# Phase 1 of a transformer block: the normalised input turned by DMA transposes of 16-bit planes in place of TensorE transposes

## The chip, the cores and the metric

The kernel runs on one core of one Trainium2 chip. The metric is the time of one execution on the device in microseconds (us), as the median of the runs shown. A profiled execution of the same kernel gives a trace, and the views quoted below are taken from it. PE is TensorE (PEld its weight loads), DVE is VectorE, ACT is ScalarE, POOL is GpSimd and SP is SyncE, whose queue issues most of the DMAs.

## What is computed

A block with 2048 tokens of width 640, 32 heads of 20 features, and a condition vector `c`:

```python
sa, ca, ga, sb, cb, gb = silu(c) @ w_mod, cut into six rows of 640
h = layernorm(x) * (1 + ca) + sa
q, k, v = h @ wqkv
phi(t) = concat(softmax(t @ w_phi), softmax(-(t @ w_phi)))      # per head
o = phi(q) (phi(k)^T v) / (phi(q) sum(phi(k)) + 1e-6)
x = x + ga * (o @ wo)
h = layernorm(x) * (1 + cb) + sb
out = x + gb * (relu(h @ w1 + b1)**2 @ w2 + b2)
```

The change is in the first line with `h`: in how the normalised x, tokens on the partitions, becomes h with its features on the partitions, as the products with wqkv need it.

## The kernel before, in words

All products are made in fp32r with both factors split into a high and a low part, and three products per pair (`three`, line 84). The tokens lie in 16 tiles of 128, worked on in eight pairs j of 256.

Phase 1 makes k, v and q of all tokens and sums phi(k)^T v. A first stretch, ordered by hand, deals with pairs 0 and 1 of tokens as far as their normalised x and h (lines 147 to 700). The loop of lines 713 to 761 then runs over the tiles t = 2 to 13, where j, i = divmod(t, 2). In each round TensorE makes k of the tile (`proj("k", t)`, line 718), v (line 727), in even rounds the sums of the two tiles before (`do_kv`, lines 729 and 730), and q (line 746; the q of the last four tiles comes later). A projection is 30 matmuls, 15 of them 384 columns wide and then 15 of 256: for each of the five chunks d of the features, three. The loop for the 384 columns already runs over all five chunks (lines 403 to 405), so a projection needs the last chunk of h after 12 matmuls.

Beside that, the loop readies the next pair, j + 1. `load_x` loads it two pairs ahead (line 716). `ln_parts` (line 331) normalises it in place in the tile `xb`, in the even round, in three steps: ACT sums the rows, ACT sums the squares with POOL working out the factors (lines 338 and 343 to 345), and ACT scales the two halves of the tile (line 348). Then `t1` (line 383) makes h of the pair: `t_in` (line 355) lets TensorE turn two blocks of 128 x 128 per chunk into the PSUM bank `tp`, and `t_out` (line 365) has ACT scale and shift them into a row `hfa` (line 368), ACT write the high part `hT` (line 369) and DVE the low part (line 88). Chunks 0 and 1 are turned at the end of the even round (line 756), chunks 2 and 3 in the odd round between v and q (line 742), chunk 4 inside q of the odd round (line 746). In three of these rounds `t1` also takes `more`: a block of a modulation row is turned on TensorE as well (`mod_turn`, line 300). For pair 7 the places are other ones, as tiles 12 and 13 make no q in the loop: line 720, line 530 by way of line 732, and line 727.

In this loop only TensorE's order is that of the program (`pe = tc.manual_schedule(engines={ET_.PE})`, line 711). What ACT, DVE, POOL and SP do is ordered by the compiler's planner, which works with its own estimate of each operation's time. `issue_after` binds some of it: `k_norm` of a round follows the DVE work written before it (line 743), and in odd rounds `q_chain` (spread, exponentials and sums of q) follows the low part of chunk 4 (`DONE[1]`, line 751). Each engine, and SP with its DMAs, works its queue in order: an instruction that waits holds all behind it.

Buffers that matter: rows of the tag `s3` (three of them, line 48) hold `junk` of `ln_parts` and `hfa`; the tiles `x0` and `x1` hold the normalised pairs alternately; `h0` and `h1` hold h.

Phase 2 (attention and the product with wo, lines 766 to 1221) and phase 3 (the MLP, from line 1224) are not touched.

Of the kernel before, what the change touches and what calls it, by code (L numbers as in the profile page):

```python
# [8 lines left out]
F32 = mybir.dt.float32  # L9
F32R = mybir.dt.float32r  # L10
I32 = mybir.dt.int32
AF = mybir.ActivationFunctionType
ALU = mybir.AluOpType
AX = mybir.AxisListType

P = 128
# [5 lines left out]
NT = S // P  # L22
NC = D // P
# [28 lines left out]
def kernel(  # L52
# [19 lines left out]
    nc = tc.nc  # L72
# [44 lines left out]
    def row(tag, name):  # L117
        return (pc if tag in ("s3", "s4") else mem).tile([P, D], F32, tag=tag, name=name, bufs=BUFS[tag])
# [19 lines left out]
    def tp(name):  # L138
        return psA.tile([P, 512], F32, tag="tp", name=name)
# [69 lines left out]
    raw, WM, RV, XB = {}, {}, {}, {}  # L209
# [18 lines left out]
    def flat(e):  # L228
        return e.rearrange("p s d -> p (s d)")
# [101 lines left out]
    def ln_parts(xt, nm, spare=None):  # L331
        sm = small([P, 2], "sm", f"sm{nm}")
        sq = small([P, 2], "sq", f"sq{nm}")
        nb = small([P, 2], "nb", f"nb{nm}")
        for i in range(2):
            same = spare[i] if spare else xt[:, i] if nm[0] == "a" else row("s3", f"same{nm}_{i}")
            nc.scalar.activation(same, xt[:, i], AF.Identity, accum_out=sm[:, i : i + 1])
        nc.gpsimd.tensor_scalar(sm, sm, -1.0 / D, None, op0=ALU.mult)
        yield
        for i in range(2):  # L340
            junk = spare[i] if spare else row("s3", f"junk{nm}_{i}")
            nc.scalar.activation(junk, xt[:, i], AF.Square, bias=sm[:, i : i + 1], accum_out=sq[:, i : i + 1])
        nc.gpsimd.tensor_scalar(sq, sq, 1.0 / D, EPS, op0=ALU.mult, op1=ALU.add)
        nc.gpsimd.tensor_tensor(sq, sq, mhalf, op=ALU.pow)
        nc.gpsimd.tensor_tensor(nb, sm, sq, op=ALU.mult)
        yield
        for i in range(2):
            nc.scalar.activation(xt[:, i], xt[:, i], AF.Identity, bias=nb[:, i : i + 1], scale=sq[:, i : i + 1])
        yield

    def layer_norm(xt, nm, spare=None):
        for _ in ln_parts(xt, nm, spare):
# [2 lines left out]
    def t_in(xn, d, p):  # L355
        for i in range(2):
            nc.tensor.transpose(p[:, i * P : (i + 1) * P], xn[:, i, d * P : (d + 1) * P], ident)  # L357
# [23 lines left out]
    DONE = []  # L381

    def t1(j, *ds, more=None):
        if 0 in ds:
            HT[j] = ht(f"hT{j}", j)
        p = tp(f"ta{j}_{ds[0]}")
        for k, d in enumerate(ds):
            t_in(XB[j], d, p[:, 256 * k : 256 * k + 256])
        if more:
            mod_turn(more[0], p[:, 256:], 4)  # L390
        for k, d in enumerate(ds):
            t_out(cols_a, HT[j], d, f"a{j}", p[:, 256 * k : 256 * k + 256])
        DONE[:] = newest(ET_.Activation), newest(ET_.DVE)
        if more:
            mod_sum(*more)
# [126 lines left out]
    def wo_weights(*gs):  # L522
# [4 lines left out]
        6: lambda: mod_turn(2, tp("mc2"), 0, 1, 2, 3),  # L527
        8: lambda: mod_turn(3, tp("mc3"), 0, 1, 2, 3),
        10: lambda: mod_turn(4, tp("mc4"), 0, 1, 2, 3),
        12: lambda: t1(NT // 2 - 1, 2, 3),  # L530
    }
    gate_a = const.tile([P, NC], F32, name="gate_a")
    gate_b = const.tile([P, NC], F32, name="gate_b")
# [179 lines left out]
    for t in range(2, NT - 2):  # L713
        j, i = divmod(t, 2)
        if i == 0 and j < NT // 2 - 2:
            load_x(j + 2)
        PK[t] = row("s2", f"k{t}")
        to_sb(proj("k", t), PK[t])
        if t == NT - 4:
            t1(j + 1, 0, 1)  # L720
        norm = j + 1 if i == 0 and t < NT - 4 else j + 2 if t == NT - 5 else None
        if norm:
            if not i:
                parts = ln_parts(XB[norm], f"a{norm}")
            with tc.issue_after(newest(ET_.Activation)):
                next(parts)
        p = proj("v", t, (1, 0, lambda: t1(j + 1, 4)) if t == NT - 3 else None)
        if i == 0:
            do_kv(t - 2)
            do_kv(t - 1)  # L730
            if t in AFTER_KV:
                AFTER_KV[t]()
        v_out(t, p)
        if norm and not i:
            next(parts)
        EK[t] = tok2("k", f"ek{t}")
        spread(PK[t], EK[t], f"k{t}")
        exps(EK[t])
        if norm and not i:
            next(parts)  # L740
        if i and t < NT - 4:
            t1(j + 1, 2, 3)
        with tc.issue_after(newest(ET_.DVE)):
            k_norm(EK[t], t)
        if t < NT - POSTPONED:
            do_q(t, (1, 3, lambda: t1(j + 1, 4, more=LAST_COL.get(t))) if i else None)
            if norm and i:
                with tc.issue_after(newest(ET_.Activation)), tc.issue_after(DONE[0]):
                    next(parts)
            if i:  # L750
                with tc.issue_after(DONE[1]):
                    q_chain(t)
            else:
                q_chain(t)
        if i == 0 and t < NT - 4:
            t1(j + 1, 0, 1)
        if t == NT - 6:
            parts = ln_parts(XB[j + 2], f"a{j + 2}")
            with tc.issue_after(newest(ET_.Activation)):
                next(parts)  # L760
        SIDE[t]()
# [941 lines left out]
```

## Time and profile before

| what | value |
|---|---|
| time, median of 3 runs | 766.31 us (765.49 to 766.42) |
| the profiled execution's own time | 766.05 us |
| its span, first to last instruction | 764.3 us |
| granted TensorE clock | 1.000 |
| TensorE's busy share of the span | 99% |
| the loop of phase 1 (tiles 2 to 13) in the span | about 52 to 224 us |

The span is what the views cut up; the 1.75 us between it and the profiled execution's own time lie around it. A row of the timeline gives start, length, engine, line, operation and how many instructions were merged. In the grouped views the mean length of one instruction stands in ns. A row of the view of a line has the shortest, the median and the longest duration.

### The profile page before, as it was taken

The page shows a single profiled execution, that of the slowest core. Times are in us where ns is not written, and L with a number is a line of the kernel's source. Part 1 is how long each engine was busy: PE and PEld are TensorE (multiplying, and loading weights), DVE is VectorE, ACT ScalarE, POOL GpSimd, SP SyncE. Part 2 cuts the span into 40 slices and gives each one's busy share as a digit, 9 for nine tenths or more (in the row PEclk, how much of TensorE's full clock was granted, in tenths as well). Part 3 has the DMA queues.
Part 4 walks back from the last instruction along what each step waited for, and adds up shares of the span by engine and source line. Part 5 has one row for each costly group of instructions (what it writes and reads, how often), then busy time and mean ns, then how long its engine had stood idle before and what let it go on. Part 6 is the DMA issues. An engine that isn't in the chain of part 4 may idle for free.

```text
span 764.3 us, 15303 instructions
## 1 busy us (share of the span) xinstructions
PE 758.5 (99%) x5968; PEld 739.7 (97%) x5968; DVE 593.9 (78%) x1083; ACT 435.6 (57%) x972; POOL 144.9 (19%) x301
## 2 busy tenths in 40 slices
PE   9999999999999999999999999999999999999997
PEld 8999999999999989988999999999999999999997
DVE  6598897988999899999655667876767666685666
ACT  5766756677853364546776647465563645536331
POOL 3001101001100255432101000231321313213110
PEclk9999999999999999999999999999999999999999
DMA  8811431343332345223366466996766759767460
GB/s 322 329 61 78 138 104 54 104 136 112 126 104 93 109 150 188 72 87 104 122 194 221 120 227 236 283 334 209 224 166 207 232 179 268 199 184 204 126 184 35
DMA packets 51505, 126.69 MB, mean 166 GB/s; under 512 B 6684, under 2 KB 7457, under 8 KB 51433
## 3 DMA queue, kind: packets, MB, share of 16 engines
q1 hardware_dynamic: 34098, 84.65, 32.8%
q0 software_dynamic: 14752, 35.76, 16.9%
q10 hardware_dynamic: 2583, 5.30, 1.8%
q8 instruction: 47, 0.77, 0.5%
q14 instruction: 25, 0.20, 0.1%
HBM read 95.70 MB, written 29.89 MB: 164 GB/s over the span
## 4 chain that ended last, share of the span: by engine, by line
PE 91%; DVE 7%; DMA 1%; issue 0%; SPq 0%; ACT 0%; DVEq 0%
PE up L78 24%; PE acc L78 18%; PE pq L78 9%; PE pk L78 9%; PE pv L78 9%; PE pwo L78 6%; PE acc3x L78 5%; PE kvp L450 3%; PE te L920 1%; DVE dn L878 1%; DVE scr L876 1%; DVE ezb L900 1%; PE tb L357 1%; PE ta L357 1%; DVE ot L88 1%; PE foldq L280 1%
## 5 line engine op out<-in xcount | busy, mean ns | idle before, releaser
L78 PE MATMUL up<-h,w 128*128 128x256 f32 x1640 | 206.4, 278 | 0.0
L78 PEld LDWEIGHTS up<-h,w 128*128 128x128 f32 x1640 | 196.1, 188 | 0.0
L1255 ACT ACTIVATE ft<-up,b_t 128x256 f32<-128x256 f32 x104 | 49.1, 472 | 113.8 <-PE up L78 113.2
L78 PE MATMUL acc<-w,ra 128*128 128x384 f32 x452 | 97.4, 335 | 0.0
L1256 DVE TENSOR_TENSOR ft<-ft 128x256 f32<-128x256 f32 x104 | 44.1, 424 | 48.4 <-ACT ft L1255 46.8
L78 PE MATMUL pwo<-wo,ot 128*128 128x256 f32 (+3 forms) x512 | 80.5, 312 | 0.1
L78 PEld LDWEIGHTS pwo<-wo,ot 128*128 128x128 f32 (+1 forms) x512 | 74.4, 188 | 3.2 <-issue 2.7
L78 PE MATMUL pq<-wq,hT 128*128 128x384 f32 (+1 forms) x480 | 75.2, 312 | 0.0
L78 PEld LDWEIGHTS acc<-w,ra 128*128 128x128 f32 x452 | 72.7, 188 | 0.8 <-DVE ra L88 0.5
L78 PE MATMUL pk<-wk,hT 128*128 128x384 f32 (+1 forms) x480 | 72.7, 308 | 0.0
L78 PE MATMUL pv<-wv,hT 128*128 128x384 f32 (+1 forms) x480 | 71.7, 307 | 0.0
L78 PEld LDWEIGHTS pq<-wq,hT 128*128 128x128 f32 x480 | 71.1, 188 | 0.6 <-issue 0.2
L78 PEld LDWEIGHTS pk<-wk,hT 128*128 128x128 f32 x480 | 70.5, 188 | 0.4 <-issue 0.2
L78 PEld LDWEIGHTS pv<-wv,hT 128*128 128x128 f32 x480 | 70.1, 188 | 0.0
L88 DVE TENSOR_TENSOR ra<-ft,ra 128x384 fp32r<-128x384 f32 (+2 forms) x86 | 36.8, 449 | 32.6 <-ACT ra L1279 19.3
L1365 POOL DMA_DIRECT2D ring_a<-td_a x34 | 18.3, 539 | 126.1 <-PE acc L78 100.4
L1279 ACT ACTIVATE ra<-ft 128x384 fp32r<-128x384 f32 x48 | 25.2, 526 | 28.4 <-DVE ft L1256 22.4
L78 PE MATMUL acc3x<-w,ra 128*128 128x256 f32 x231 | 39.8, 278 | 0.0
L78 PEld LDWEIGHTS acc3x<-w,ra 128*128 128x128 f32 x231 | 37.2, 188 | 0.2 <-DVE ra L88 0.2
L1270 DVE TENSOR_TENSOR ft<-ft 128x128 f32<-128x128 f32 x136 | 33.4, 287 | 1.2
L441 DVE TENSOR_REDUCE sk<-ek 128x64 f32<-128x1280 f32 x16 | 23.7, 1484 | 12.4 <-ACT ek L436 10.8
L884 POOL TENSOR_TENSOR dn<-dn,rs_q 128x32 f32<-128x32 f32 x32 | 20.2, 630 | 66.7 <-DVE dn L878 66.4
(270 smaller groups left out, 1412.6 us busy)
## 6 DMA issues: line engine op xcount, KB each, us to landing
ring_c<-td_c POOLq DMA_DIRECT2D x34, 384.0 KB, 4.2
ring_a<-td_a POOLq DMA_DIRECT2D x34, 384.0 KB, 4.1
ring_b<-td_b POOLq DMA_DIRECT2D x34, 256.0 KB, 4.0
esp<-eq SPq DMA_DIRECT2D x12, 640.0 KB, 3.0
el<-esp SPq DMA_DIRECT2D x12, 640.0 KB, 3.9
rw<-in_w SPq DMA_DIRECT2D x23, 320.0 KB, 2.9
wm<-in_w_mod SPq DMA_DIRECT2D x20, 320.0 KB, 3.3
xb<-in_x SPq DMA_DIRECT2D x8, 640.0 KB, 4.2
```

The lines of the kernel that those rows point to most:

```text
L78: nc.tensor.matmul(o, a, b, start=first and i == 0, stop=last and i == len(terms) - 1, skip_group_check=skip,)
L88: (eng or nc.vector).tensor_tensor(out_lo, full, hi.bitcast(F32), op=ALU.subtract)
L280: nc.tensor.matmul(p[g // 3][:, (g % 3) * 120 : (g % 3) * 120 + n], r, bd_t[:120, g * 120 : g * 120 + n], start=True, stop=True,)
L357: nc.tensor.transpose(p[:, i * P : (i + 1) * P], xn[:, i, d * P : (d + 1) * P], ident)
L441: nc.vector.tensor_reduce(s, heads(flat(e)), axis=AX.X, op=ALU.add)
L450: nc.tensor.matmul(kvp[g // 4][64 * c : 64 * c + 64, a : a + 2 * n].rearrange("p (s n) -> p s n", s=2), v[:, u], e[:, :, o : o + n], start ...
L884: nc.gpsimd.tensor_tensor(dn[:, s], dn[:, s], rs[:, 1 - s], op=ALU.mult)
L1255: nc.scalar.activation(r, p, AF.Relu, bias=b1_t[:, f : f + 1])
L1256: nc.vector.tensor_tensor(r, r, r, op=ALU.mult)
L1270: nc.vector.tensor_tensor(t[:, o], t[:, a], t[:, b], op=op)
L1279: nc.scalar.activation(a[:, 0, :3], t[:, :3], AF.Copy)
L1365: nc.gpsimd.dma_start(RING[j, n, r], TD[n][r].bitcast(F32R))
```

## The change

`ln_parts` of a pair that belongs to phase 1's loop (pairs 2 to 7) ends with `by_dma`. The normalised tile is read as 16-bit numbers, and POOL copies the lower and the upper halves of all numbers into two planes for each of the two token tiles: four copies of 128 x 640 numbers with a step of two. Four DMA transposes from SP's queue then turn each plane, 128 tokens x 640 features, into five blocks of 128 x 128, written back over the normalised tile. In `t1` POOL joins the two planes of a chunk into a row `hfa`, two copies of 128 x 256 numbers with a step of two in what is written, and `t_out` works on that row in place, reading SBUF where it read PSUM. TensorE turns nothing of x in the loop. `t1` for chunks 0 and 1 moves from the end of the even round to the odd round, behind the copies of k; pair 7's chunks 0 to 3 all move to the odd round t = 13. The blocks of the modulation rows are still turned on TensorE, in a PSUM tile of their own and ahead of the chunk's work.

```diff
+    def by_dma(j, xt):
+        raw = flat(xt).bitcast(U16)
+        halves = raw.rearrange("p (i d h) -> p i h d", i=2, h=2)
+        turned = raw.rearrange("p (h b t) -> p h b t", h=2, b=NC)
+        planes = [row("s3", f"pl{j}_{i}").bitcast(U16).rearrange("p (h d) -> p h d", h=2) for i in range(2)]
+        for i in range(2):
+            for h in range(2):
+                nc.gpsimd.tensor_copy(planes[i][:, h], halves[:, i, h])
+        for i in range(2):
+            for h in range(2):
+                nc.sync.dma_start_transpose(turned[:, h, :, i * P : i * P + P], planes[i][:, h])
+        TURNED[j] = turned
...
     def t1(j, *ds, more=None):
+        if more:
+            mod_turn(more[0], tp(f"mc{j}")[:, 256:], 4)
         if 0 in ds:
             HT[j] = ht(f"hT{j}", j)
-        p = tp(f"ta{j}_{ds[0]}")
-        for k, d in enumerate(ds):
-            t_in(XB[j], d, p[:, 256 * k : 256 * k + 256])
-        if more:
-            mod_turn(more[0], p[:, 256:], 4)
-        for k, d in enumerate(ds):
-            t_out(cols_a, HT[j], d, f"a{j}", p[:, 256 * k : 256 * k + 256])
+        for d in ds:
+            hf = row("s3", f"hfa{j}_{d}")[:, :256]
+            for h in range(2):
+                nc.gpsimd.tensor_copy(hf.bitcast(U16).rearrange("p (t h) -> p h t", h=2)[:, h], TURNED[j][:, h, d])
+            t_out(cols_a, HT[j], d, f"a{j}", hf, hf)
...
-        if t == NT - 4:
+        if i:
             t1(j + 1, 0, 1)
+            if t == NT - 3:
+                t1(j + 1, 2, 3)
...
-        if i == 0 and t < NT - 4:
-            t1(j + 1, 0, 1)
```

More of the change, by code (lines that the diff above doesn't have):

```diff
@@ L11 @@
 I32 = mybir.dt.int32
+U16 = mybir.dt.uint16
 AF = mybir.ActivationFunctionType
@@ L348, in ln_parts @@
             nc.scalar.activation(xt[:, i], xt[:, i], AF.Identity, bias=nb[:, i : i + 1], scale=sq[:, i : i + 1])
+        if nm[0] == "a":
+            by_dma(int(nm[1:]), xt)
         yield
+    TURNED = {}
+    def by_dma(j, xt):
[10 more added lines that the diff above has]
+        TURNED[j] = turned
     def layer_norm(xt, nm, spare=None):
@@ L529 @@
         10: lambda: mod_turn(4, tp("mc4"), 0, 1, 2, 3),
-        12: lambda: t1(NT // 2 - 1, 2, 3),
     }
```

## The prediction

> **What bounds the kernel now.** I read the page first, then the stretch between two pairs (tiles 4 and 5, which make ready pair 3) by engine, then TensorE's timeline in it.
>
> ```profile
> span 764.3 us, 15303 instructions
> PE 758.5 (99%) x5968; PEld 739.7 (97%) x5968; DVE 593.9 (78%) x1083; ACT 435.6 (57%) x972; POOL 144.9 (19%) x301
> PEclk9999999999999999999999999999999999999999
> ```
>
> TensorE is busy from end to end, at full clock. So a microsecond taken off TensorE comes off the time, as long as nothing else becomes late. That is the question of this change, and it is decided in the loop. The next two views are of one round of it, by engine, and of the tile `ta` (the transposes) alone: busy times of PE, PEld, DVE, ACT, POOL in the first, of PE, PEld, ACT in the second.
>
> ```profile
> 81.90:111.70 29.80, 29.80 (x236) 29.58 (x235) 26.81 (x35) 19.57 (x44) 2.84 (x4) 1.00 0.35 114
> 81.90:111.70 29.80, 1.58 (x10) 1.16 (x10) 2.60 (x5) 1.00 0.35 114
> ```
>
> DVE is at 26.81 of 29.80 us: nearly as full as TensorE. POOL is almost empty. TensorE's own order there:
>
> ```profile
> 81.79 4.46 PE L78 MATMUL pk<-wk,hT 128*128 128x384 f32 x30
> 86.09 4.46 PE L78 MATMUL pv<-wv,hT 128*128 128x384 f32 x30
> 90.48 2.54 PE L450 MATMUL kvp<-ek,vt 128*64 128x120 f32 x44
> 92.95 4.65 PE L78 MATMUL pq<-wq,hT 128*128 128x384 f32 x30
> 97.44 0.60 PE L357 MATMUL ta<-ident,xb 128*128 128x128 f32 x4
> 97.79 4.62 PE L78 MATMUL pk<-wk,hT 128*128 128x384 f32 x30
> 102.25 4.47 PE L78 MATMUL pv<-wv,hT 128*128 128x384 f32 x30
> 106.56 0.60 PE L357 MATMUL ta<-ident,xb 128*128 128x128 f32 x4
> 106.91 3.22 PE L78 MATMUL pq<-wq,hT 128*128 128x384 f32 x18
> 109.97 0.38 PE L357 MATMUL ta<-ident,xb 128*128 128x128 f32 x2
> 111.60 0.68 PE L78 MATMUL pk<-wk,hT 128*128 128x384 f32 x3
> ```
>
> **Taken off TensorE.** From one pair's first k to the next is 111.60 - 81.79 = 29.81 us. A projection with no transposes at it takes 86.09 - 81.79 = 4.30, the sums of kv 92.95 - 90.48 = 2.47; six projections and one kv are 28.27. Left over are 1.54 us. The projection ahead of kv is 0.09 over 4.30 (90.48 - 86.09), and I leave as much for the one behind it; both stay. The ten transposes with what they disturb therefore cost 1.54 - 0.18 = 1.36 us per pair, bounded by their weight loads alone (1.16) and by all of it (1.54). Six pairs: **-8.2 us** (-7.0 to -9.2). The modulation blocks still turned (lines 305 and 306) stay as they are. The pair's period without transposes is 29.81 - 1.36 = 28.45 us.
>
> **The deadline.** Count from a pair's first k (81.79 = 0). The next pair's k would start at 28.45. The last chunk of h is needed after 12 of its 30 matmuls; 384 columns take 4.30 x 384 / 9600 = 0.172 us each, so 2.06 later: **30.5**. Before, this chain was ACT's scaling, a short turn on TensorE, ACT and DVE, with time to spare. Now it holds POOL, SP and the DMA engines.
>
> **The chain, step by step.** Its beginning and its end have rows (start, length; shortest/median/longest for the lines):
>
> ```profile
> 93.25 1.74 ACT L348 ACTIVATE xb<-xb,nba,sqa 128x640 f32<-128x640 f32 x2 [0.95 <-POOL nba L345]
> L368 ACT ACTIVATE hfa<-ta,cols_a x30: 555/564/578, 68.3 to 222.4; 128x256 f32<-128x256 f32 x30
> L369 ACT ACTIVATE hT<-hfa x40: 407/417/431, 20.9 to 223.1; 128x256 fp32r<-128x256 f32 x40
> 109.30 0.76 DVE L88 TENSOR_TENSOR hT<-hfa,hT 128x256 fp32r<-128x256 f32 x2
> 111.59 0.42 DVE L88 TENSOR_TENSOR hT<-hfa,hT 128x256 fp32r<-128x256 f32 x1
> ```
>
> *Start.* The first half is scaled at 93.25 + 0.87 = 94.12, that is 12.3; the second 0.87 later, hidden by POOL's first copies.
>
> *Four copies into planes.* No row shows such a copy. The rows around it on POOL:
>
> ```profile
> L489 POOL MEMSET rwo<- x5: 627/632/637, 152.8 to 188.7; 128x640 f32 x5
> L338 POOL TENSOR_SCALAR sma<-sma x6: 217/226/579, 58.4 to 192.2; 128x2 f32<-128x2 f32 x6
> L882 POOL TENSOR_SCALAR dd<-dd x16: 289/290/1410, 59.3 to 359.2; 128x32 f32<-128x32 f32 x16
> L884 POOL TENSOR_TENSOR dn<-dn,rs_q x32: 248/254/1481, 258.2 to 361.2; 128x32 f32<-128x32 f32 x32
> L884 POOL TENSOR_TENSOR dn<-dn,rs_q 128x32 f32<-128x32 f32 x32 | 20.2, 630 | 66.7 <-DVE dn L878 66.4
> ```
>
> Writing 640 numbers takes 0.63 us: the lower end. With one input, 30 numbers more cost 290 - 226 = 64 ns, 2.1 ns each, so 640 would take 1.6 us: the upper end. I take 0.9, near the memset, which has the length of this copy. To it comes a wait: L884 has a median of 254 ns and a mean of 630, with a longest of 1481, so on average it stood 0.38 us; I take 0.3. Four copies: 4 x 1.2 = **4.8 us** (2.5 to 7.6).
>
> *Four DMA transposes* of 160 KB each. No row shows one. Nearest are an ordinary store of 640 KB and small loads of 150 KB (KB each, us to landing):
>
> ```profile
> esp<-eq SPq DMA_DIRECT2D x12, 640.0 KB, 3.0
> rwo<-in_wo SPq DMA_DIRECT2D x10, 150.0 KB, 2.6
> ```
>
> If the four run together like one plain transfer: 3.0 us. If each waits for the one before: 4 x 2.6 = 10.4. I take **6 us**, between them, since SP must issue four and the last two wait for POOL's last copies. [...]
>
> *Ten copies that join*, 256 numbers each, all ahead of the last chunk: by the memset's rate 256 / 640 x 0.63 = 0.25, by the other row 0.22 + 254 x 2.1 ns = 0.75. I take 0.42 and the same wait of 0.3: **7.2 us** (2.5 to 10.5).
>
> *Last chunk through ACT and DVE:* 0.56 + 0.42 + 0.42 = 1.4, the same as before but now at the chain's end; and 1.2 for standing behind others there (half an ACT operation of 0.8 and a whole one of DVE): **2.6 us** (1.4 to 4). That ACT reads SBUF instead of PSUM I count at nothing: the same ACT group, off TensorE's path unless late.
>
> Sum: 12.3 + 4.8 + 6 + 7.2 + 2.6 = 32.9, **2.4 us after the deadline**. TensorE's order is fixed, so it stands and does nothing else. Per pair that is 2.4 - 1.36 = +1.04. This holds for pairs 2 to 6. Pair 7 is normalised earlier against its use:
>
> ```profile
> 203.21 1.72 ACT L348 ACTIVATE xb<-xb,nba,sqa 128x640 f32<-128x640 f32 x2
> 223.80 2.41 PE L78 MATMUL pk<-wk,hT 128*128 128x384 f32 x13
> ```
>
> There 204.1 + 4.8 + 6 + 7.2 + 2.6 = 224.7 against 223.80 - 1.36 + 2.06 = 224.5: on time, -1.2. Total 5 x 1.04 - 1.2 = **+4.0 us**.
>
> **What else is queued.** POOL waits at a join until the DMA has landed; behind it stand only `ln_parts` of the next round and a few memsets, not due yet. DVE is worse off: `k_norm` and `q_chain` of the odd round are bound behind the low parts of chunks 3 and 4. These ended at 110.06 and 112.01 (28.3 and 30.2); they move to about 31 to 33, while 26.81 us of DVE's work per pair must still fit. The wait of TensorE lengthens the period to about 30.9, so this is covered in the forecast; it isn't if the chain comes in time (third rival). On SP the transposes stand in a queue that already stops:
>
> ```profile
> 91.08 12.08 SPq L314 DMA_DIRECT2D wm<-in_w_mod  x3
> ```
>
> The third of these loads waits for its buffer until DVE has freed it. It is written in the program behind the round's transposes, so I count nothing; if it is put ahead of them, they go out at 103.2 instead of about 97, 6 us later.
>
> **Rivals.**
>
> 1. *In time.* POOL's copies at memset's rate and the DMA like one plain store: 12.3 + 3.7 + 3.0 + 5.5 + 2.6 = 27.1, well before 30.5 (waits of 0.3 included). Then all 8.2 us are gained: **758**, up to 763 with a little left on DVE. For it speaks the nearly empty POOL, against it that every unknown must be near its lower end. This ends on the other side; it decides at a chain 1.36 us past the deadline, 31.9.
>
> 2. *Later still.* The four DMAs one after the other (10.4), POOL's copies at the one-input row's rate (7.6 and 10.5): 12.3 + 7.6 + 10.4 + 10.5 + 2.6 = 43.4, 12.9 past the deadline, 5 x 11.5 - 1 = +57 at worst; with only the DMAs so, 37.3 and +26; halfway to that, with SP's load ahead now and then, **780 to 795**. The row of 12.08 us on SP speaks for it. [...]
>
> 3. *DVE becomes the bound.* The chain is in time, but POOL's 14 copies per pair hold DVE up. What the rows show is the other direction: POOL's operation of 254 ns took up to 1481 while DVE worked. Would DVE be stopped as well?
>
> ```profile
> L443 DVE TENSOR_TENSOR ek<-ek,sk x16: 1480/1486/1493, 45.7 to 243.6; 128x1280 f32<-128x1280 f32 x16
> ```
>
> Not so far: the long one never varies, but POOL had little to do beside it. DVE's operations with two inputs in this round are 20:
>
> ```profile
> L296 DVE SCALAR_TENSOR_TENSOR wm<-wm,cs,wm 128x640 f32<-128x640 f32 x4 | 3.5, 880 | 0.0
> L433 DVE TENSOR_TENSOR ek<-k,mxk 128x640 f32<-128x640 f32 x4 | 3.1, 818 | 0.0
> L433 DVE TENSOR_TENSOR eq<-q,mxq 128x640 f32<-128x640 f32 x4 | 3.0, 802 | 0.0
> L443 DVE TENSOR_TENSOR ek<-ek,sk 128x1280 f32<-128x1280 f32 x2 | 3.0, 1488 | 0.0
> L88 DVE TENSOR_TENSOR hT<-hfa,hT 128x256 fp32r<-128x256 f32 x6 | 2.3, 417 | 0.0
> ```
>
> If a quarter of them meets a copy under way (4 x 0.9 + 10 x 0.42 = 7.8 us of 28.45) and waits 0.3 to 0.5 us, that is 1.5 to 2.5: DVE needs 28.3 to 29.3, and 0.5 to 1.4 us of gain are left per pair, **759 to 763**; with DVE idle behind a low part for another microsecond, up to **768**. [...]
>
> 4. *It doesn't do what it says:* the transposes on TensorE are gone by the diff, so this can only be the order on SP, counted in 2.
>
> **How the numbers follow.** The profiled execution took 766.05 us (span 764.3), 0.26 under the median of 766.31; both give the same change. Forecast 766.3 + 4.0 = **770.3 us**. Chances: late by about this much (768 to 778) 0.30; in time, gain nearly whole (757 to 763) 0.27; near break-even, by DVE or a chain just late (763 to 768) 0.17; late by more (778 to 795) 0.18; over 795 0.08. Within 0.2%, 1.5 us, is about what a measurement can't tell from no change. Of the break-even case 0.08 lies under, 0.08 within and 0.01 over. Faster 0.35, same 0.08, slower 0.57. The range runs from the whole gain, 758, to 790.
>
> **What would show it.** Right: per pair a pause of 1 to 4 us on TensorE at the first k of pairs 3 to 6, ended by DVE or ACT on `hT`, none at pair 7, and joins on POOL released by the transposes' DMA. The plane copies should stand near 0.9, the joins near 0.4, the DMAs land some 6 us after the last plane. Wrong: no pause and a period near 28.5 (rival 1); pauses over 5 us (2); DVE without idle time and long DVE operations beside POOL's copies (3). A DMA transpose of over 4 us each, or under 1, breaks the middle step.

## The result, and the profile after

The changed kernel takes 785.16 us (median of five runs, 784.04 to 786.42) against 766.32 us before (five runs, 765.49 to 766.89): ratio 1.0249, 95% interval 1.0234 to 1.0264. It is slower, by 18.8 us where 4.0 were forecast. The profiled execution took 786.42 us, the longest of the five; its span is 784.7 - 764.3 = 20.4 us over the one before.

The page of the changed kernel, two lines of its head and the weight loads of k (busy time, mean ns of one | idle time just before them and what ended most of it); below it the same group in the view of groups of the kernel before:

```profile
span 784.7 us, 15359 instructions
PE 766.1 (98%) x5908; PEld 739.8 (94%) x5908; DVE 601.6 (77%) x1083; ACT 437.1 (56%) x972; POOL 196.7 (25%) x385
L79 PEld LDWEIGHTS pk<-wk,hT 128*128 128x128 f32 x480 | 76.4, 207 | 20.1 <-DVE hT L89 13.4
```

```profile
L78 PEld LDWEIGHTS pk<-wk,hT 128*128 128x128 f32 x480 | 70.5, 188 | 0.4 <-issue 0.2 <-ACT hT L369 0.2
```

Sixty matmuls are gone, as meant, and yet PE is busy 7.6 us longer than before (758.5). The weight loads of k show both reasons. They wait 20.1 us in place of 0.4, mostly for DVE's low part of h. And one of them lasts 207 ns in place of 188, though each does the same as before. The loads overlap one another (480 x 207 ns are 99.4 us, in 76.4 of busy time), so 480 x 19 ns is not a time lost. The granted clock of the whole execution, 0.988 in place of 1.000, has the cause: TensorE stood at half its clock in four stretches of 17.1 us together, which cost at most 8.5 us. The last 1.58 us of the span are at half clock too, but TensorE's last matmul had ended 2.5 us before them. The account nearly closes: 19.7 + 8.5 - 8.2 forecast for the turns = 20.0 us, against the 20.4 between the spans.

Where it happens is seen by cutting out the k projections that follow each pair's change (window, length, busy PE, PEld, DVE, ACT, POOL, then the granted clock): pairs 2 to 6 with the k of their first tile, pair 7 with its two k, which stand together. The row of the kernel before is pair 2's.

```profile
81.23:89.99 8.76, 7.16 (x32) 5.60 (x31) 6.68 (x11) 3.60 (x8) 1.21 (x3) 0.82 0.43 135
114.40:121.62 7.22, 5.89 (x32) 4.21 (x31) 5.68 (x9) 3.71 (x10) 1.31 (x4) 1.00 0.47 142
146.46:155.06 8.60, 6.50 (x33) 5.68 (x31) 7.40 (x11) 3.52 (x9) 1.01 (x3) 0.80 0.41 136
179.93:186.33 6.40, 5.17 (x33) 4.17 (x31) 5.12 (x8) 2.94 (x8) 0.42 (x2) 1.00 0.38 123
211.13:223.29 12.16, 8.07 (x32) 6.52 (x31) 9.52 (x15) 8.57 (x19) 7.17 (x13) 0.72 0.64 173
238.97:251.78 12.81, 11.19 (x63) 10.16 (x61) 10.28 (x14) 4.60 (x10) 0.78 (x1) 0.87 0.19 54
```

```profile
81.79:86.09 4.30, 4.30 (x32) 4.30 (x31) 4.01 (x7) 1.62 (x3) 0.00 (x0) 1.00 0.52 176
```

Each length less 4.30 is what a pair lost there (pair 7: less 8.69, as 232.49 - 223.80 before). Length times what the clock lacks is the clock's share; the rest is waiting:

| pair | forecast | lost | by the clock | by waiting |
|---|---|---|---|---|
| 2 | 2.4 | 4.46 | 1.58 | 2.88 |
| 3 | 2.4 | 2.92 | 0 | 2.92 |
| 4 | 2.4 | 4.30 | 1.72 | 2.58 |
| 5 | 2.4 | 2.10 | 0 | 2.10 |
| 6 | 2.4 | 7.86 | 3.40 | 4.46 |
| 7 | 0 | 4.12 | 1.67 | 2.45 |
| sum | 12.0 | 25.8 | 8.4 | 17.4 |

In pair 6 the clock's share is set too high and the waiting too low, by up to 0.7 us, since TensorE's weight loads also waited 1.4 us while the clock stood at half. Between these projections the changed kernel is faster, as meant, but by 0.97 to 1.27 us per pair, 6.9 in all, not 8.2. From the loop's first k (52.39, before 51.98) to the kv products after pair 7 (251.78, before 232.49) that makes 25.8 - 6.9 = 18.9 us. Of the other 1.5, 0.4 lie ahead of the loop and 1.1 behind it; these weren't followed up.

What TensorE's timeline of the k in pair 2 shows of its waits is only a part:

```profile
81.23 1.20 PE L79 MATMUL pk<-wk,hT 128*128 128x384 f32 x6
82.80 2.50 PE L79 MATMUL pk<-wk,hT 128*128 128x384 f32 x8 [0.37 <-ACT hT L387]
86.53 3.66 PE L79 MATMUL pk<-wk,hT 128*128 128x384 f32 x16 [1.23 <-DVE hT L89]
```

The eight matmuls of the second row would take some 1.3 us; more short waits hide in its 2.50, and the weight loads show them. After them the clock is at exactly one half from 86.82 to 90.23 us: 3.41 us, 1.7 lost, on top of the wait. Pair 3 waited as long (2.92 us for 2.88) and kept the full clock, so between these two the length of the waits doesn't decide.

What differs can be read from the trace. The four stretches at half clock begin at 86.82, 151.67, 216.52 and 243.83 us and last 3.41, 3.41, 6.83 and 3.41 us; between their beginnings lie 19, 19 and 8 times 3.413 us. So in this trace the clock changes only on a grid of 3.413 us, which the waits between don't shift. These are the windows of that grid in which most of each pair's waiting lies, and two stretches at half clock behind such windows (columns as above; the fourth figure is the time in which weight loads ran):

```profile
83.40:86.82 3.42, 2.19 (x9) 1.19 (x9) 3.00 (x5) 1.20 (x3) 0.00 (x0) 1.00 0.69 192
86.82:90.23 3.41, 3.41 (x17) 3.41 (x17) 3.41 (x5) 0.49 (x2) 0.00 (x0) 0.50 0.00 0
117.54:120.95 3.41, 2.17 (x14) 1.67 (x14) 3.38 (x6) 0.63 (x2) 0.00 (x0) 1.00 0.51 180
148.26:151.67 3.41, 1.49 (x7) 1.11 (x8) 3.38 (x7) 1.26 (x3) 0.00 (x0) 1.00 0.56 192
182.39:185.80 3.41, 2.18 (x15) 1.76 (x15) 3.38 (x6) 0.54 (x2) 0.00 (x0) 1.00 0.38 152
213.11:216.52 3.41, 0.98 (x6) 0.35 (x4) 1.60 (x2) 3.35 (x9) 3.27 (x8) 1.00 0.42 104
216.52:223.35 6.83, 6.02 (x23) 5.42 (x24) 6.48 (x10) 3.24 (x6) 3.63 (x6) 0.50 0.69 194
240.42:243.83 3.41, 1.78 (x8) 0.89 (x7) 2.56 (x5) 1.70 (x4) 0.00 (x0) 1.00 0.37 152
```

The four windows with the fewest weight loads, 0.35, 0.89, 1.11 and 1.19 us (pairs 6, 7, 4 and 2), are the four that half clock follows; after those with 1.67 and 1.76 us (pairs 3 and 5) the clock stays. The 19 traces of this case, cut on their own grids, have 4228 windows at full clock. Half clock follows all 24 with under 1.20 us of weight loads and none of the 4184 with over 1.55; in between, 10 of 20. So pair 3's 2.92 us of waiting, cut in two by the grid (weight loads of 2.15 us in 114.12 to 117.54, then the 1.67), were free of this cost, and pair 2's 2.88 us, more of them inside one window (2.49 us in 79.99 to 83.40, then the 1.19), cost 1.7 us more.

Now the chain that was forecast, in pair 2 (first k at 52.39): POOL, then SP, then DVE's low parts.

```profile
64.57 2.71 POOL L363 COPY pl<-xb 128x640 uint16<-128x640 uint16 x4 [1.02 <-ACT xb L349]
71.65 1.46 POOL L409 COPY hfa<-xb 128x256 uint16<-128x256 uint16 x2 [4.36 <-DMA xb<-pl]
73.52 1.73 POOL L409 COPY hfa<-xb 128x256 uint16<-128x256 uint16 x4 [0.40 <-DMA xb<-pl]
80.63 1.81 POOL L409 COPY hfa<-xb 128x256 uint16<-128x256 uint16 x4 [5.38 <-DVE hT L89]
65.99 6.11 SPq L366 DMA_TRANSPOSE xb<-pl  x4
80.15 0.42 DVE L89 TENSOR_TENSOR hT<-hfa,hT 128x256 fp32r<-128x256 f32 x1
86.11 0.36 DVE L89 TENSOR_TENSOR hT<-hfa,hT 128x256 fp32r<-128x256 f32 x1
```

Three chunks are joined by 75.25, 22.9 us after the first k and sooner than forecast. Then POOL stands for 5.38 us: the joins of chunks 3 and 4 need a row of `s3`, there are three, and the first comes free when DVE's low part of chunk 0 ends, at 80.57. That one is late because ACT takes chunk 0 only at 77.46, behind exponentials and the copies of v. DVE's last low part ends at 86.47.

Pair 7 (POOL's factors, planes and first join, then SP):

```profile
212.84 2.19 POOL L409 COPY hfa<-xb 128x256 uint16<-128x256 uint16 x4 [4.34 <-DVE hT L89]
215.11 0.19 POOL L344 TENSOR_SCALAR sqa<-sqa 128x2 f32<-128x2 f32 x1
218.55 2.91 POOL L363 COPY pl<-xb 128x640 uint16<-128x640 uint16 x4 [1.23 <-ACT xb L349]
230.23 2.04 POOL L409 COPY hfa<-xb 128x256 uint16<-128x256 uint16 x1 [8.77 <-DMA xb<-pl]
220.77 1.94 SPq L366 DMA_TRANSPOSE xb<-pl  x1
226.21 0.33 SPq L498 DMA_DIRECT2D esp<-eq  x1
226.63 1.68 SPq L366 DMA_TRANSPOSE xb<-pl  x1
```

Its factors (215.11) stand in POOL's queue behind a join of pair 6 that waits 4.34 us for a row, so its planes start only at 218.55; k, late by then itself, starts 20.4 us after that (238.97), where 19.7 lay between the first half's scaling and k before. Then its transposes stand on SP behind a store `esp<-eq` at 226.21, 3.5 us after the first transpose had left SP, and the first join comes 8.77 us after the last plane, where pair 2 needed 4.37.

### The profile page after: what moved, and what is told of

It is laid out like the page before. It is cut to its first block, busy times and chain, and to the rows that moved or that the text cites. A ratio compares the mean times of both kernels' runs of the same rounds, so it can differ in the third digit from the quotient of the medians.

```text
span 784.7 us, 15359 instructions
## 1 busy us (share of the span) xinstructions
PE 766.1 (98%) x5908; PEld 739.8 (94%) x5908; DVE 601.6 (77%) x1083; ACT 437.1 (56%) x972; POOL 196.7 (25%) x385
## 4 chain that ended last, share of the span: by engine, by line
PE 68%; DVE 16%; ACT 6%; issue 5%; DMA 2%; POOL 1%; SPq 1%; DVEq 0%; POOLq 0%; ACTq 0%
PE up L79 23%; PE acc L79 17%; PE pwo L79 5%; PE acc3x L79 5%; PE pk L79 4%; PE pq L79 4%; PE pv L79 3%; DVE sk L459 2%; DVE ek L451 2%; DVE eq L451 1%; PE te L937 1%; DVE dn L895 1%; DVE scr L893 1%; DVE ezb L917 1%; PE tb L375 1%
## 5 line engine op out<-in xcount | busy, mean ns | idle before, releaser
L79 PE MATMUL pk<-wk,hT 128*128 128x384 f32 (+1 forms) x480 | 86.1, 335 | 12.0 <-DVE hT L89 8.4
L79 PEld LDWEIGHTS pk<-wk,hT 128*128 128x128 f32 x480 | 76.4, 207 | 20.1 <-DVE hT L89 13.4
L409 POOL COPY hfa<-xb 128x256 uint16<-128x256 uint16 x60 | 34.0, 619 | 47.5 <-DMA xb<-pl 28.4
L1296 ACT ACTIVATE ra<-ft 128x384 fp32r<-128x384 f32 x48 | 25.2, 526 | 28.4 <-DVE ft L1273 22.4
L444 ACT ACTIVATE k<-pk 128x384 f32<-128x384 f32 (+1 forms) x32 | 13.6, 436 | 46.0 <-PE pk L79 46.0
```

The source lines that it names most:

```text
L79: nc.tensor.matmul(o, a, b, start=first and i == 0, stop=last and i == len(terms) - 1, skip_group_check=skip,)
L409: nc.gpsimd.tensor_copy(hf.bitcast(U16).rearrange("p (t h) -> p h t", h=2)[:, h], TURNED[j][:, h, d])
L444: nc.scalar.activation(t[:, a:b], p[h][:, : b - a], AF.Copy)
L1296: nc.scalar.activation(a[:, 0, :3], t[:, :3], AF.Copy)
```

## The experiments

Three theories at first. **O**, order and rows: each step is cheap, but in-order queues and the three rows of `s3` hold the chunks up. **D**: the DMA transposes are too long. **P**: POOL's copies and DVE's operations hold each other up. From the run with the stores issued by ACT on, O is sharpened to "the queues": an instruction that waits holds all behind it, as the store at 226.21 us held pair 7's transposes on SP. Times are medians, ratios against the kernel before on the same chip.

**One row for the joins of a call of `t1`** (the changed kernel, otherwise as it is).

```diff
+        both = row("s3", f"hfa{j}_{ds[0]}")
-        for d in ds:
-            hf = row("s3", f"hfa{j}_{d}")[:, :256]
+        for k, d in enumerate(ds):
+            hf = both[:, 256 * k : 256 * k + 256]
```

> The changed kernel, with the chunks of one call of t1 side by side in one row of tag s3 (two of 256 numbers) instead of a row each; nothing else. Theory O (order and rows: the DMA and GpSimd's copies are early enough; the joins of chunks 3 and 4 wait for a row that DVE's low part of an earlier chunk has to free, and ACT and DVE take up the chunks late): the joins of chunks 3 and 4 no longer wait for DVE's hT, some 2 us per pair come back, 773 to 779 us. Theory D (the DMA transposes take too long): 785 as before. [...]

778.82 us, 1.0162 (1.0145 to 1.018): 12.7 us over the kernel before in place of 18.8. But the weight loads of k still wait 18.8 us in place of 20.1, so the rows were little of the waiting. The clock was more: 6.8 us at half in this profile in place of 17.1, worth up to 5.1 us. Pair 7's joins are the latest.

**The changed kernel without its four DMA transposes** (the joins read the normalised tile as it lies; h isn't turned).

```diff
-        for i in range(2):
-            for h in range(2):
-                nc.sync.dma_start_transpose(turned[:, h, :, i * P : i * P + P], planes[i][:, h])
-        TURNED[j] = turned
+        TURNED[j] = raw.rearrange("p (d t h) -> p h d t", d=NC, h=2)
```

> The changed kernel with the four DMA transposes per pair left out: the joins read the normalised tile as it lies, so h is not turned (this part of the computation is changed). All copies on GpSimd and all work on ACT and DVE stay. Theory D: the cause is gone, 757 to 763 us. Theory O: the joins come about 5 us earlier per pair, but ACT and DVE still take the chunks up late and rows are still short: 775 to 785. Theory P: 780 to 785.

775.70 us, 1.013 (1.0105 to 1.0155). Without a single transpose in the chain the kernel is still 9.6 us slower than before. D falls as the main cause: at most half of the loss hangs on the DMAs, and of the waiting at k much less, as 17.3 of the 20.1 us stay.

**The kernel before with `t1` at the changed kernel's places**, turned by TensorE.

```diff
-        if t == NT - 4:
+        if i:
             t1(j + 1, 0, 1)
+            if t == NT - 3:
+                t1(j + 1, 2, 3)
...
-        if i == 0 and t < NT - 4:
-            t1(j + 1, 0, 1)
```

> The kernel before, TensorE turning x as it did, with nothing but the places of t1 moved as in the change (chunks 0 and 1 behind the copies of k in the odd round, pair 7's chunks 0 to 3 all in t = 13). Theory O in its strong form (the place of t1 alone makes the chunks late): 772 to 785 us. Theories D and P, and O in its weak form (the place only hurts with the joins' waits): 766 to 769.

770.88 us, 1.006 (1.0045 to 1.0075). The later places alone cost 4.7 us, with no DMA and no copy on POOL.

**The kernel before with POOL's 14 copies per pair beside it**, their results unused.

```diff
+        planes = [row("s3", f"pl{j}_{i}").bitcast(U16).rearrange("p (h d) -> p h d", h=2) for i in range(2)]
...
+                nc.gpsimd.tensor_copy(planes[i][:, h], halves[:, i, h])
...
+                nc.gpsimd.tensor_copy(to[:, h], planes[0][:, h, 64 * d : 64 * d + 256])
```

> The kernel before with GpSimd's 14 copies per pair added and used by nobody (four of the normalised halves into planes, ten of 256 numbers from plane to plane); TensorE turns x as before. Theory P: DVE, at 26.8 of 29.8 us, is held up by 1.5 to 2.5 us per pair and more behind it, 772 to 785 us. Theories O and D: DVE's operations with two inputs get longer, but its idle time takes that up, 766 to 769.

776.27 us, 1.0127 (1.011 to 1.0144). This was no clean test: the planes took two of the three rows of `s3`, and the waits view shows who stood (us, times, longest):

```profile
ACT hfa L382 <- DVE hT L89: 8.6, 12, 2.4
PE ta L371 <- ACT hfa L382: 7.0, 4, 4.3
```

**The same copies in a buffer of their own.**

```diff
+    scratch = pc.tile([P, 576], F32, name="scratch")
...
-                nc.gpsimd.tensor_copy(planes[i][:, h], halves[:, i, h])
+                nc.gpsimd.tensor_copy(plane, halves[:, i, h])
```

> The run with GpSimd's 14 copies per pair added to the kernel before, once more, but the copies go to a scratch tile of their own and take no row of tag s3 away from the chunks. [...] Theory O (rows and order): what e4_pool lost came from the two rows that its planes held; 766 to 770 us.

767.42 us, 1.0012 (1.0002 to 1.0021). 84 copies cost 1 us in all, and P falls as the main cause. They do lengthen DVE's work, by 5.3 us in all (599.2 busy in place of 593.9), but in this kernel DVE's idle time takes that up. All but that 1 us of the 10.1 us of the run before came from the rows.

**The changed kernel with `t1` at the kernel before's places.**

```diff
-        if i:
+        if t == NT - 4:
             t1(j + 1, 0, 1)
...
+        if i == 0 and t < NT - 4:
+            t1(j + 1, 0, 1)
```

> The changed kernel with t1 at the places of the kernel before (chunks 0 and 1 at the end of the even round, pair 7's as before); planes, DMA transposes and joins as in the change. If the places cost what e3_moved showed by themselves (4.7 us), 779 to 782 us. If they were only put there because the data come later, and ACT now waits at the chunks with the copies of k behind it, 785 to 795.

785.49 us, 1.0238 (1.0205 to 1.0271). The places that were good for TensorE's turns don't help chunks that come later; the 4.7 us above can't simply be taken off.

**Pairs 3 to 7 normalised in the odd round ahead**, with the shared rows and the earlier places.

```diff
-        norm = j + 1 if i == 0 and t < NT - 4 else j + 2 if t == NT - 5 else None
+        norm = j + 1 if t == 2 else j + 2 if i and t < NT - 4 else None
...
-        if t == NT - 6:
+        if i == 0 and t < NT - 5:
             parts = ln_parts(XB[j + 2], f"a{j + 2}")
```

> The changed kernel with the rows of e1_rows, the places of e7_places, and pairs 3 to 7 normalised one round earlier (in the odd round ahead, as the change does for pair 7 alone), so that the transposes have some 11 us more. Theory that lateness against TensorE's deadline is all of the loss: no pauses at k, 757 to 763 us, faster than before. Theory P, or rows still short (the row of junk now lies between the chunks' rows): 766 to 775.

776.96 us, 1.0131 (1.0114 to 1.0148): some 2 us better than the shared rows alone. **And with one row for the `junk` of the squares:**

```diff
-            junk = spare[i] if spare else row("s3", f"junk{nm}_{i}")
+            junk = spare[i] if spare else one
```

> As e8_early, with one row instead of two for what the sums of squares write (junk), so that three rows go round without a chunk waiting for another chunk's. Theory of lateness and rows: 757 to 762 us, at least 1 us under e8_early if rows still wait there. Theory P: the same as e8_early, 766 to 775.

775.72 us, 1.0121 (1.0101 to 1.014). A whole round more for the chain, and of the 12.7 us with shared rows 9.3 are left. The waits at k do fall, from 18.8 to 12.1 us, but TensorE stands 10.2 us at half clock in place of 6.8. In this trace some pairs run without a wait, others lose all the more, each behind something that waits at the head of a queue: on SP a load `ga_b<-gate` that waits for its store to land (store at 148.20 us, load at 158.19, transposes from 158.62).

**The shared rows (first experiment), the stores `esp<-eq` issued by ACT.**

```diff
-            nc.sync.dma_start(ESP[t], flat(e))
+            nc.scalar.dma_start(ESP[t], flat(e))
```

> The changed kernel with the rows of the first experiment (the joins of one call of t1 in one row), and the stores esp<-eq issued by ScalarE, which has just written eq, in place of SP. In the run of that first experiment (778.8 us) SP held pair 7's transposes from 215.6 to 226 us because a store esp<-eq stood between them and waited for ScalarE's exponentials. Theory of the queues (an instruction that waits holds the ones behind it): pair 7's joins come some 5 us earlier, the pause in front of it shrinks by 3 to 6 us: 773 to 776 us. Theory that the latency of the transposes themselves decides: nothing, 778 to 780 us.

782.0 us, 1.0207 (1.0183 to 1.0231): a miss, 3 us slower. The timeline shows why the gap stayed: another DMA waits at the same place on SP, and ACT itself now idles 2.96 us until a store `esp` has ended (SP's rows first):

```profile
218.93 3.79 SPq L366 DMA_TRANSPOSE xb<-pl  x2
225.78 0.33 SPq L315 DMA_DIRECT2D wm<-in_w_mod  x1
226.21 2.53 SPq L366 DMA_TRANSPOSE xb<-pl  x2
227.29 0.47 ACT L438 ACTIVATE vt<-pv 128x360 f32<-128x360 f32 x1 [2.96 <-DMA esp<-eq]
```

**The early normalisation with the same stores on ACT.**

```diff
-            nc.sync.dma_start(ESP[t], flat(e))
+            nc.scalar.dma_start(ESP[t], flat(e))
```

> The kernel that normalises pairs 3 to 7 one round earlier, with shared rows for joins and for the junk of the squares (775.7 us), and in addition the stores esp<-eq issued by ScalarE. Theory of the queues: pair 7, the last place where this kernel pauses behind such a store, loses 2 to 4 us: 771.5 to 774 us; the pauses of pair 2 (POOL's queue) and of pair 5 (SP's queue behind the store of the gate) stay. Theory of the latency: 775 to 777 us.

773.6 us, 1.0088 (1.0071 to 1.0105): 2.1 us better, as the queues would have it.

**And the gate row a round later, the next factors behind the joins of chunks 2 and 3.**

```diff
-        7: lambda: (spread_row(0, gate_a, ga_b), mod_mac(4, 3)),
-        8: lambda: mod_mac(4, 4),
+        7: lambda: mod_mac(4, 3),
+        8: lambda: (spread_row(0, gate_a, ga_b), mod_mac(4, 4)),
```

> The same, and two more places in which something waits at the head of a queue are taken away: the store and load of the gate row (ga_b<-gate) are issued one round later, so that SP does not hold pair 5's transposes for 10 us, and the factors of the pair after next are computed behind the joins of chunks 2 and 3 in POOL's queue instead of ahead of them. Theory of the queues: all pairs as its undisturbed ones, 29.1 us in place of 30.4 in the kernel before, so that the time falls below the kernel before: 758 to 766 us. If something other than the queues keeps the time up (the extra work of POOL and DVE, the clock): 770 us or more.

772.53 us, 1.0078 (1.0063 to 1.0093): still over the kernel before, so the forecast of 758 to 766 missed. But its pairs 3 to 6 now run nearly as meant: the four rounds are shorter than before by 1.28, 1.31, 0.60 and 1.43 us. The window of pair 3 (columns as above), and TensorE's kv products that bound a round, of this kernel and of the one before:

```profile
117.10:146.17 29.07, 29.07 (x231) 28.85 (x230) 29.00 (x35) 19.82 (x46) 12.20 (x18) 1.00 0.43 125
125.80 2.54 PE L470 MATMUL kvp<-ek,vt 128*64 128x120 f32 x44
154.86 2.54 PE L470 MATMUL kvp<-ek,vt 128*64 128x120 f32 x44
```

```profile
120.30 2.54 PE L450 MATMUL kvp<-ek,vt 128*64 128x120 f32 x44
150.67 2.54 PE L450 MATMUL kvp<-ek,vt 128*64 128x120 f32 x44
```

29.06 us per pair in place of 30.37: 1.31 gained, with no wait of TensorE and the full clock. DVE is busy 29.00 of 29.07 us. From kv to kv, 36 operations on either side keep it busy 28.99 us here and 26.88 in the kernel before (`eq<-q` lasts 1106 ns on average in place of 820), so nothing more can come off this round unless DVE gets less to do. What is lost lies at pair 2 (normalised no earlier than before) and pair 7.

**Pairs 3 to 6 by DMA, pairs 2 and 7 by TensorE, in the same frame.**

```diff
+    BY_DMA = (3, 4, 5, 6)
...
+        by_pe = j not in BY_DMA
```

> The kernel of the three repaired queues (772.5 us), with the chunks of pairs 2 and 7 turned by TensorE again at the kernel before's places, and pairs 3 to 6 turned by DMA. In that kernel's trace pairs 3 to 6 ran without pauses at 29.1 to 29.6 us each, against 29.8 to 30.4 us in the kernel before, while pair 2 stood 8 us and pair 7 some 3 us behind. Theory of the queues: the four clean pairs keep about 1 us each and the two others cost nothing: 761 to 765 us. If the transposes cost the kernel something that those pairs do not show (POOL's and DVE's added work, the clock): 766 us or more.

764.99 us, 0.998 (0.9971 to 0.9989): 1.1 us, or 0.2%, under the kernel before. **Its control, all pairs by TensorE:**

```diff
-    BY_DMA = (3, 4, 5, 6)
+    BY_DMA = ()
```

> The control for the run beside it: the same frame (normalisation a round early, the stores esp<-eq on ScalarE, the gate row a round later, a shared row for the junk of the squares), with all pairs turned by TensorE. Theory of the queues: the frame itself is worth nothing, 765 to 768 us, so that the mixed kernel's gain is the four pairs' transposes. If the frame is the gain: as the mixed kernel.

770.13 us, 1.0045 (1.0032 to 1.0057). The frame costs 4 us, the DMA turns of four pairs win 5.1. That is 1.3 a pair, though it isn't all TensorE's work: the control also waits 4.0 us at k, the mixed kernel 2.1. Neither leaves the full clock.

**The mixed kernel with the next pair's squares behind the last chunk in ACT's queue.**

```diff
-            with tc.issue_after(newest(ET_.Activation)):
-                next(parts)
...
+                for _ in range(2):
+                    with tc.issue_after(newest(ET_.Activation)), tc.issue_after(DONE[0]):
+                        next(parts)
```

> The mixed kernel (pairs 3 to 6 turned by DMA, 764.99 us) with the squares and the scaling of the pair after next behind the last chunk of the pair on hand in ScalarE's queue. In the mixed kernel ScalarE's squares for pair 3 (78.90 and 80.97 us) stand ahead of pair 2's last chunk, and TensorE waits 1.24 us for it at 85.61. Theory of the queues: that pause and its like in the other rounds go, 1 to 3 us: 762 to 764 us. If the order on ScalarE is not what delays that chunk: 765 us again, or more where pair 3's planes now come too late.

769.23 us, 1.0032 (1.002 to 1.0045): the wait at pair 2 is gone as expected (kv at 90.04 in place of 92.00 us), and the time rises all the same. Pair 5's transposes now find SP taken (SP, then ACT), and later in the profile TensorE stands 3.4 us at half clock, where the mixed kernel had none:

```profile
143.68 0.38 SPq L329 DMA_DIRECT2D gate<-gate_a  x1
155.06 0.33 SPq L330 DMA_DIRECT2D ga_b<-gate  x1
155.48 2.97 SPq L368 DMA_TRANSPOSE xb<-pl  x2
164.16 0.60 ACT L388 ACTIVATE hfa<-hfa,cols_a 128x256 f32<-128x256 f32 x1 [5.06 <-POOL hfa L420]
```

**The same with pair 7 by DMA too.**

```diff
-    BY_DMA = (3, 4, 5, 6)
+    BY_DMA = (3, 4, 5, 6, 7)
```

> The same with pair 7 turned by DMA too (pairs 3 to 7; pair 2 by TensorE). TensorE's work falls by another 1.3 us, as by the control. In the kernel of three repaired queues pair 7's transposes stood behind loads on SP that wait for a free buffer (217.6 us), and its chunks came late by some 3 us. Theory of the queues: that remains, 763 to 768 us, slower than the run beside it; by the transposes' work alone it would be 1.3 us faster than it.

773.93 us, 1.0094 (1.0079 to 1.0109): 4.7 us worse than the run beside it. The loss at pair 7 stays, as expected; that it would end at 768 at most did not hold.

**The load of the gate row behind pair 5's transposes.**

```diff
+        with tc.issue_after(TURNS[-1]):
+            load_gate(0, ga_b)
```

> The kernel with pair 3 to 6 turned by DMA and the next pair's squares behind the chunks (769.23 us), with the load ga_b<-gate issued behind pair 5's four transposes. In that kernel's trace SP stands from 143.68 to 155.06 us at that load, which waits for the store of the gate to land; pair 5's planes are ready by 148.1, its transposes start at 155.48, and its chunks are 5 us late for ScalarE (164.16 us, 5.06 us of idle time); up to there the kernel is 3 us ahead of the kernel before (the kv product at 147.69 against 150.67). Theory of the queues: pair 5 becomes clean, the lead of 3 us grows to 4 or 5, and the time falls to 761 to 765 us. If pairs 5 and 6 are late for another reason: 767 to 770 us.

767.22 us, 1.0011 (1.0002 to 1.0019): 2.0 us better than with the load ahead (769.23), and pair 5's round falls from 33.66 us (kv at 147.69 and 181.35) to 31.19 (148.33 and 179.52). So that load was a cause, but not all of it: 761 to 765 was missed, since pair 6's round stayed at 33.3 (30.8 before), with 3.4 us at half clock in it. **And pair 6 by TensorE:**

```diff
-    BY_DMA = (3, 4, 5, 6)
+    BY_DMA = (3, 4, 5)
```

> The same with pair 6 turned by TensorE too, so that pairs 3 to 5 alone go by DMA. Pair 6's round also brings wo's weights to ScalarE, DVE and SP. Theory of the queues: TensorE has 1.3 us more work; if pair 6 by DMA pauses in the run beside it (0.9 us for DVE's low part in the earlier one), this kernel is the same or up to 2 us faster; if pair 6 by DMA is clean, it is 1.3 us slower.

766.95 us, 1.0012 (1.0 to 1.0024): the same. Pair 6 by DMA wins nothing there and loses nothing.

Side by side, with the weight loads' waits at k and the time at half clock from each profile:

| kernel | us over the kernel before | waits at k | at half clock |
|---|---|---|---|
| changed kernel | 18.8 | 20.1 | 17.1 |
| shared rows | 12.7 | 18.8 | 6.8 |
| no transposes | 9.6 | 17.3 | 6.8 |
| shared rows, earlier normalisation, one row for `junk` | 9.3 | 12.1 | 10.2 |
| the same, three queues repaired | 6.1 | 9.4 | 6.8 |
| pairs 2 and 7 by TensorE | -1.1 | 2.1 | 0 |

So the waiting goes with earlier planes and freer queues, and with leaving out the two pairs that were still late; rows and DMAs alone hardly change it. The time at half clock is no fixed share of it, and a difference of 1 or 2 us between two of these kernels can be the clock alone.

## Why the forecast was right in sign and wrong in size

The profiled execution lost 20.4 us where 4.0 were forecast. Of the 16.4 between them 8.4 are the clock, 5.4 are waiting over the 12.0 forecast (2.9 in pairs 2 to 6, 2.5 in pair 7), 1.3 are saving that didn't come, and 1.5 lie outside the loop.

**TensorE's saving, -1.36 per pair: nearly held.** 1.31 in the undisturbed pair of a later kernel, 0.97 to 1.27 in this one.

**The deadline and the chain's lateness, 2.4 us per pair for pairs 2 to 6: nearly right as a wait, for other reasons.** Waiting alone was 3.0 on average (14.9 us for five, 12.0 forecast). Step by step in pair 2: start 12.2 (12.3 forecast). Planes 2.71 (4.8). From the last plane to the first join 4.37 (6). The ten joins 5.0 in work (7.2), but ended at 30.05 us (30.3 forecast) through 5.38 us of waiting for a row that no step had. From there to the last low part 4.0 (2.6), the upper bound. Three terms were too dear, and a wait that wasn't in the sum ate what they left: that the sum came out near is luck. In the run with shared rows 18.8 of the 20.1 us of waiting at k stay, so that wait wasn't the only one the sum lacked.

**"TensorE's order is fixed, so it stands and does nothing else": this is the step that failed most.** A late microsecond was priced at a microsecond. In the trace four windows with such waits are also followed by a clock of 0.50, three times for 3.41 us and once for 6.83: 8.4 us lost in these projections. The forecast gave the clock no price, as the kernel before ran its loop at 1.00 throughout. No long pause was needed for the loss: TensorE's rows in the loop of the changed kernel have one of 2.39 us at most, 2.71 between two weight loads, and ahead of the rows from 86.82 us weight loads ran in 1.19 of the 3.42 us, with no wait over 1.55 us between two of them.

**Pair 7 "on time, -1.2": failed.** It lost 4.1 us, 2.45 of them by waiting. The time between its scaling and its k was nearly the one forecast (20.4 us for 19.7), but the chain took longer: from the first plane at 218.55 to TensorE's last wait for DVE, 243.72, are 25.2 us in place of 4.8 + 6 + 7.2 + 2.6 = 20.6. SP's store alone put 4.4 us more into the transposes' step (8.77 for 4.37). And "What else is queued" had said that `ln_parts` behind a join isn't due yet: wrong for this pair, whose factors run in the odd round behind pair 6's joins; only because k was late as well did that not cost more.

**DMA transposes, 6 us, landing about 6 us after the last plane:** each lands in 3.0 us, and the four hold SP for 1.27 us each. View of the line, and the waits view:

```profile
L366 SPq DMA_TRANSPOSE xb<-pl x24: 1207/1270/2167, 66.0 to 230.3; - x24
DMA to landing us min/median/max: 2.6/3.0/4.1
POOL hfa L409 <- DMA xb<-pl: 28.4, 11, 8.8
POOL hfa L409 <- DVE hT L89: 18.7, 7, 5.4
```

POOL's joins wait two thirds as long for rows (18.7 us) as for DMAs (28.4). The size was about right, and the run without them leaves 17.3 of the 20.1 us of waiting at k. The 640 KB of a pair, pair 2's, took about 7.5 us, from 65.99 to the join that waited for the second tile at 73.52, some 87 GB/s, planes' copies included.

**SP's load counted at nothing:** right for that load in pair 2, but other DMAs that wait on SP hold transposes in pairs 5 and 7, which the gate's load shows by 2.0 us.

**Rivals.** DVE as the bound (third) didn't come in the changed kernel, where TensorE's lateness leaves DVE time. Its price of 1.5 to 2.5 us per pair was right all the same: 2.1 in the undisturbed pair, where DVE has 0.07 us left. The 1.0 us for all copies is what they cost a kernel whose DVE has idle time. Of "later still" (second) its range held the time, 780 to 795, though by rows, queues and the clock, and not by slower copies or serial DMAs. "In time" (first) is what three of the four clean pairs show (1.28, 1.31 and 1.43 us).

**Open:** what decides on the clock between 1.20 and 1.55 us of weight loads in a window; the 1.5 us outside the loop; how much of the waiting in the changed kernel is DVE's lengthened work; and why the frame of the mixed kernel costs 4 us, of which 3.6 are longer waits at k (4.0 against 0.4). That a kernel with all six pairs clean would reach the 758 us of the first rival is argued, not shown: the best seen is 764.99.

## What to carry to other kernels

When work moves off the bottleneck onto a chain of other engines, add up the durations, and then list for each link what may wait ahead of it in the same in-order queue (here a store on SP went out 3.5 us after pair 7's first transpose had left, with the other three behind it) and how many buffers the link needs until the last reader frees them. Here the durations were cheaper than thought, and the waits in queues and for rows cost all the gain and more. TensorE, whose weight loads of k had waited 0.4 us before, lost more than its waits: where several short ones fell together into one window of 3.41 us, half clock followed, at up to 1.7 us lost per 3.41 us of it. That was 8.4 us on 17.4 of waiting, with shared rows up to 3.4 on 18.8.

## What the runs showed of the hardware that was not expected

TensorE's granted clock changed only on a grid of 3.413 us that no wait of these kernels shifted: in all 19 traces it held for whole multiples of that time. It was 0.50 after every window at full clock with under 1.20 us of weight loads, and stayed at 1.00 after every one with over 1.55. Short waits were enough for it: the 1.19 us of loads ahead of 86.82 us are spread over their window. GpSimd copied 16-bit numbers with a step of two fast: 0.73 us for 128 x 640, 0.48 for 128 x 256 (views of the lines in the changed kernel; the row of L433 is the kernel before's).

```profile
L363 POOL COPY pl<-xb x24: 715/727/1316, 64.6 to 220.7; 128x640 uint16<-128x640 uint16 x24
L409 POOL COPY hfa<-xb x60: 469/481/2038, 71.7 to 238.0; 128x256 uint16<-128x256 uint16 x60
L433 DVE TENSOR_TENSOR ek<-k,mxk 128x640 f32<-128x640 f32 x32 | 25.1, 819 | 0.8 <-PE kvp L450 0.7
L451 DVE TENSOR_TENSOR ek<-k,mxk 128x640 f32<-128x640 f32 x32 | 28.5, 920 | 0.9 <-PE kvp L468 0.8
```

Where they met, both sides could lengthen: in the changed kernel two `ek<-k` from 128.75 us took 2.60 us, at a median of 0.82 each, beside plane copies of which four took 4.87 us from 128.31, where pair 2's four took 2.71. Beside the longest join, 2038 ns at 230.23 us, two `ek<-k` kept to 1.55 us together. On average `ek<-k` went from 819 ns before to 920 here. The run with the copies in a buffer of their own prices this at 1.0 us for 84 of them, beside a DVE with idle time.
